# An attention and feed-forward stack on one core: causal tiles of 64 queries with shared products, gates in one run, q and phi k by head block

## The chip, the cores and the metric

One core of a Trainium2 chip runs the whole program. The metric is the time of one execution on the device in microseconds (us). TensorE is called PE here, VectorE DVE, ScalarE ACT, GpSimd POOL, and SyncE, which issues most DMAs, SP.

## What is computed

Four blocks in a row act on x, [2048, 512] in bf16: attention with a memory, a gated feed-forward, and both again with the same weights.

```
x = x + A(layernorm(x));  x = x + B(layernorm(x))      # twice
A: q, k, v = x wq, x wk, x wv         # 32 heads of 16; 4 segments of 512 tokens, one after the other
   a_dot = softmax(q k^T / 4, causal within the segment) v
   a_mem = phi(q) M / (phi(q) z + 1e-6)     # M, z: sums of phi(k) v and phi(k) of the segments before
   A = (g a_mem + (1 - g) a_dot) wo         # g = sigmoid(beta), by head; phi(t) = t + 1 if t > 0, else exp(t)
B: (gelu(x w_gate) * (x w_up)) w_down       # 512 -> 1792 -> 512
```

## The kernel before

A segment of 512 tokens in one pass of attention and feed-forward is a **layer** k; there are 8, k = 0 to 3 the first pass and 4 to 7 the second. The classes `Att` and `Ffn` hold a layer's work as items (q and k by head block b, v by token tile, wo, 14 gates, 14 ups, 4 downs, the memory's update). A head block is 8 heads, 128 of the 512 columns of q; its four groups of 32 partitions hold an even head in the first 16 rows and an odd head in the last 16.

**Scores.** `score_round` makes scores transposed: 128 keys on the partitions, queries in the free dimension, four heads at once in four row strips of PE. For an even head the weights are the 16 rows of k; for an odd head they are 32 rows of `kB`, a copy of k whose even rows are zero. Causal tiles are 128 queries wide: key tile ki meets the 512 - 128 ki queries from 128 ki on, 1280 columns a head, cut by `PIECES` into 5 rounds of 256 columns (`narrow` cuts 128 into 64 for even heads). A **score event** issues two rounds, which fill two pairs of PSUM banks; one exponential on ACT (L1285, 128x1024) empties a pair into a slot of `pt`; POOL zeroes the masked half of the diagonal tile in it (L1291). There are 40 rounds of four heads in a layer and 320 in all.

**Flush.** `flush_item` (L864) multiplies the probabilities of four heads of one parity by v in four column strips of PE. `vaug` holds v with a column of ones times 1/(1 - g) for the denominator. A flush takes 1280 columns and must wait for all masks of its rounds; DVE turns, divides and turns back (L879 to L897), and the slots of `pt` come free.

**Memory.** phi is exp on ACT (L648), a minimum on POOL (L666), a sum on DVE (L652), which for k sums z as well, and a DMA transpose on SP.

**Feed-forward.** A gate is four products of 512 columns. Nine of a layer's 14 are evicted to `gel_sb` by DVE or ACT (L408, L409) and get Gelu later from there (L1046), five get it straight from PSUM (L972); both need a table of ACT other than that of the exponential. DVE multiplies by the ups (L994).

**The order.** All five engines run in an order that `order` writes when the program is built. It keeps a clock for each engine with fixed costs and takes, whenever PE is free, first a score event if two bank pairs and two slots are free and ACT is about to run dry (`rounds_now`), then the open item's next product, then the ready item that is due first. Where nothing is ready it issues a filler product on the tile `warm`, whose result nobody reads. `POLICY` is a table of some forty numbers that shift due times and priorities. PE changes between three modes: row strips (scores, reading the memory), column strips (flush, update, and dense products beside them; L418) and the whole array (dense products, L421). On the chip each engine runs its list in order and waits on semaphores alone.

**Storage.** q, k and `kB` have 3 sets, each of a whole layer, and a layer's projections wait until the scores and phi of the layer three before are done. For k < `kb_dve` = 4 DVE makes kB with a mask (L591); after that SP copies 16 rows of each of four strips by DMA, 4 DMAs a head block (L588). xn, the normalized rows, have 4 buffers and are turned by DMA on SP (L384), or by PE (L509) for three norms.

Of the kernel before, what the change touches and what calls it, by code (L numbers as in the profile page):

```python
# [38 lines left out]
ROUNDS = 5  # L39
STEPS = 8 * ROUNDS  # L40
PIECES = [[(0, 0, 256, 0)], [(0, 256, 256, 0)], [(1, 128, 256, 0)], [(3, 384, 128, 0), (1, 384, 128, 128)],
          [(2, 256, 256, 0)]]
NO_DIAG = 1


def narrow(pieces, par):

    if par:
        return pieces
    return [(ki, q0 + o, min(n, 64) if n == P else n, c0 + o) for ki, q0, n, c0 in pieces  # L50
            for o in ((0, P // 2) if n == P else (0,))]
# [5 lines left out]
SETS = 3  # L57

URGENT, SOON, NORMAL = -4.0, -1.5, 0.0
XN_BUFS = 4  # L60
# [4 lines left out]
POLICY = dict(  # L65
    flush_wait=152.105, piece_slack=40.738, kb_slack=10.905, mem_slack=-2.348, margin=2.56, qk_due=0.594,
    e_q=-0.77, e_k=1.073, exp_slack=-18.49, e_slack=11.096, phi_slack=6.459, gelu_slack=-0.034, act_evict=5.372,
    first_evict=-0.382, gate_step=0.0, up_due=1.256, up_step=0.012, down_due=3.948, down_step=1.013,
    upd_due=-0.62, v0_due=1.254, x1_at=0.158, x2_at=5.744, x3_at=0.964, x3_load=17.129, cut_slack=-0.231,
    direct=5, gelu_tiles=1, phi_pool=0, kb_dve=4, rounds=2, early=0.939, starve=0.658, ahead=0.286, near=-3.652,  # L70
    cap=7, soon=1.448, am_slack=1.081, mem_wait=0.156)
# [11 lines left out]
class Engine:  # L83
# [4 lines left out]
    def __init__(self, overlap=0.0):  # L88
        self.free, self.overlap, self.jobs, self.table = 0.0, overlap, [], "exp"
        self.only, self.rival, self.port = None, None, 0.0  # L90

    def post(self, ready, slack, *steps, table=None, taken=None):

        self.jobs.append((ready, slack, steps, table, taken if taken is not None else []))

# [12 lines left out]
    def serve(self, now):  # L108

        self.jobs = [j for j in self.jobs if not j[4]]  # L110
        jobs = [j for j in self.jobs if not self.only or j[3] in (None, self.only)]
        if not jobs:
            return False
        start = max(self.free, min(j[0] for j in jobs) + self.LATENCY)
# [5 lines left out]
        self.jobs.remove(job)  # L120
        t = ready
# [18 lines left out]
class Clocks:  # L140
# [4 lines left out]
    SWITCH = 0.097  # L145

    def __init__(self):
# [7 lines left out]
        self.ev = {}  # L155

# [19 lines left out]
    def serve(self):  # L176

        again = True
        while again:
            again = False  # L180
            while self.later and self.later[0][0] <= self.pe:
                heapq.heappop(self.later)[2]()
                again = True
            for w in list(self.waiting):
                if w[0]():
                    self.waiting.remove(w)
                    w[1]()
                    again = True
            first = min(self.engines, key=lambda e: max(e.free, min((j[0] for j in e.jobs), default=1e9)))
            again |= first.serve(self.pe) or any(e.serve(self.pe) for e in self.engines)  # L190
# [52 lines left out]

class Box:
# [9 lines left out]
class Policy:  # L254
    def __init__(self, values):
        self.__dict__.update(values)


def order(pol, nc, cst, seg, wrk, psp, A_x, A_wq, A_wk, A_wv, A_wo, A_beta, B_x, B_w_gate, B_w_up, B_w_down, out):
# [70 lines left out]
    bd = cst.tile([P, P], F32, name="bd")  # L330
    nc.gpsimd.memset(bd[:], 1.0)
    nc.gpsimd.affine_select(out=bd[:], in_=bd[:], pattern=[[-16, 8], [0, 16]], compare_op=ALU.is_ge,
                            fill=0.0, base=0, channel_multiplier=1)
    nc.gpsimd.affine_select(out=bd[:], in_=bd[:], pattern=[[16, 8], [0, 16]], compare_op=ALU.is_ge,
                            fill=0.0, base=15, channel_multiplier=-1)
    kBs = [cst.tile([P, KT, L], BF16, name=f"kB{i}") for i in range(SETS)]
    for kB in kBs[1:]:
        nc.vector.memset(kB[:], 0.0)
    mask2 = cst.tile([P, 2 * DH], F32, name="mask2")
    nc.vector.reduce_sum(out=mask2[:], in_=bd[:].rearrange("p (c n) -> p n c", c=4), axis=mybir.AxisListType.X)  # L340
    maskB = mask2[:, DH:DH + 1]

    tmp_e = cst.tile([P, H], F32, name="tmp_e")
    tmp_e2 = cst.tile([P, H], F32, name="tmp_e2")
    cden = cst.tile([P, H], BF16, name="cden")
    macc = cst.tile([P, 4, 2 * DH], F32, name="macc")
    e2x = cst.tile([P, 2, 2, 2, 4 * TPS], F32, name="e2x")
    zacc = cst.tile([P, 4], F32, name="zacc")
    vaugs = [cst.tile([P, TPS, VW + 15], BF16, name=f"vaug{i}")[:] for i in range(SETS)]
    vaugs.append(gel_sb[:].rearrange("p f l -> p (f l)")[:, 0:TPS * (VW + 15)].rearrange("p (t v) -> p t v", t=TPS))  # L350

    def by_head(va):
        return va[:, :, 0:VW].rearrange("p t (h e) -> p t h e", e=DH + 1)


    def gate_constants():
        nc.vector.tensor_scalar(out=cden[:], in0=tmp_e[:], scalar1=1.0, scalar2=None, op0=ALU.add)
        nc.vector.tensor_scalar(out=tmp_e2[:], in0=tmp_e2[:], scalar1=1.0, scalar2=None, op0=ALU.add)

    def gate_rows(half, b):  # L360
        for p in range(2):
            nc.vector.tensor_copy(
# [4 lines left out]

    def later_constants():
        def column(va):
            nc.vector.tensor_copy(out=by_head(va)[:, :, :, DH], in_=cden[:].unsqueeze(1).to_broadcast([P, TPS, H]))  # L370
            nc.vector.memset(va[:, :, VW:], 0.0)

        for n, va in enumerate(vaugs[-1:] + vaugs[:-1]):
            ck.dve.post(12.0 + 3.0 * n, NORMAL, (0.4, lambda va=va: column(va), None))
        for n in range(4):
            ck.dve.post(26.0 + 2.0 * n, NORMAL, (0.25, lambda n=n: gate_rows(*divmod(n, 2)), None))

    def turn_later(t, slack, out, in_, landed, margin=0.0):

        def told(t2):  # L380
            t3 = max(t2 + 1.4 + margin, ck.dma + 1.2)
            ck.at(t3 - 0.2, lambda: landed(t3))

        ck.sp.post(t, slack, (1.3, lambda: nc.sync.dma_start_transpose(out=out(), in_=in_()), told))  # L384
# [49 lines left out]
    class Norm:  # L434
# [4 lines left out]
        def small(self, name, width):  # L439
            return wrk.tile([P, TPS, width], F32, tag=f"{name}{self.key[0]}{self.key[1] % 2}", bufs=1, name=name)  # L440
# [34 lines left out]
        def normed(self, j, i):  # L475
            xn = seg.tile([P, D], BF16, tag=f"xn{i}", bufs=1, name="xn")
            nc.vector.tensor_scalar(out=xn[:], in0=x_sb[:, self.tt0 + j, :], scalar1=self.mv[:, j, 0:1],  # L477
# [3 lines left out]
        def row(self, j, i, ready):  # L481
# [8 lines left out]
            def told(t):  # L490
                if self.key in BY_PE:
                    items.append(self.turn_item(j, xn, t, landed))
                else:
                    turn_later(t, self.slack, lambda: self.xnT[:, :, j * P:(j + 1) * P], lambda: xn()[:], landed,
# [4 lines left out]
        def turn_item(self, j, xn, t, landed):  # L499

            ps = Psum()
            half = L // 2

            def turned():
                return ps()[:, 0:half].bitcast(BF16).rearrange("p (k t) -> p k t", t=P)

            ops = [(Clocks.MM[512] / 2, whole(lambda: nc.tensor.matmul(
                ps()[:, half:L], lhsT=warm[:], rhs=wide[:, 0:2, :], start=True, stop=True)))] * FILL
            ops += [(Clocks.MM[128], whole(lambda kt=kt: nc.tensor.transpose(  # L509
                turned()[:, kt, :], xn()[:, kt * P:(kt + 1) * P], ident[:]))) for kt in range(KT)]  # L510
            return Item(-0.5, lambda: t + Engine.LATENCY <= ck.pe + FILL * Clocks.MM[512] / 2, ops,
# [21 lines left out]
    class Att:  # L533
        def __init__(self, k):
            self.k, self.s, self.tt0 = k, k % NSEG, TPS * (k % NSEG)
            self.norm = Norm(("xnTa", k), self.tt0, f"xnTa{k % 2}", NORMAL, lambda: k < 2 or ("qkv", k - 2) in ev)
            self.vaug = vaugs[(k - 1) % SETS if k else SETS]
            self.ab, self.aT, self.amT, self.n_qkv, self.n_am, self.n_num = {}, None, {}, 0, 0, 0
# [7 lines left out]
        def add_items(self):  # L546
            k, s = self.k, self.s

            def storage():
                return k <= SETS or (("scores", k - SETS) in ev and self.phi_done(k - SETS))  # L550

            def first():
                if k:
                    self.q, self.kf = (seg.tile([P, KT, L], BF16, tag=f"{n}{k % SETS}", bufs=1, name=n)
# [861 lines left out]
```

## Time and profile before

| what | us |
|---|---|
| three runs, median (lowest to highest) | 547.7 (547.62 to 548.58) |
| the profiled execution's own time | 547.77 |
| its span, first to last instruction | 546.1 |
| busy PE, DVE, ACT, POOL | 535.6, 442.4, 445.5, 278.8 |
| exponentials of the scores, 320 | 308.0 |
| masks on POOL, 320 | 184.2 |

The span leaves out what lies around the program, 1.7 us here. A row of the groups reads: line, engine, operation, tiles with shapes, count | busy us, mean ns of one | idle time before, and what ended it. Busy times overlap where an engine starts one instruction before the last has ended. A row of the chain or the timeline reads: start, length, engine, line, tiles, count; matmuls of equal shape and some unequal ones are merged, and the end of the last is modelled. A matmul in strips is counted four times, once a strip.

### The profile page before, as it was taken

How to read it: one execution, taken by the hardware profiler on the slowest of the kernel's cores; microseconds unless marked ns; L12 is line 12 of the kernel's file. 1: busy time of each engine (PE TensorE's matmuls, PEld its weight loads, DVE VectorE, ACT ScalarE, POOL GpSimd, SP SyncE). 2: the span in 40 equal slices, each digit the busy share in tenths (PEclk: the TensorE clock that was granted, in tenths of full speed). 3: DMA queues.
4: the chain of work that ended last, by engine and by line, in shares of the span. 5: the costliest groups of instructions: out<-in, count | busy, mean ns of one | idle time of the engine just before them, and what ended most of it. 6: DMA issues, size and time to landing. Idle time of an engine off the chain costs nothing.

```text
span 546.1 us, 23526 instructions
## 1 busy us (share of the span) xinstructions
PE 535.6 (98%) x10291; PEld 266.0 (49%) x10321; DVE 442.4 (81%) x880; ACT 445.5 (82%) x572; POOL 278.8 (51%) x410
## 2 busy tenths in 40 slices
PE   9999999999999999999999999999999999999997
PEld 4444444445544444444444444455454446445444
DVE  7999999779998999588987987979768796786072
ACT  5899989999999959989999899988998789910500
POOL 2687774367928847156862668724574155300000
PEclk9999999999999999999999999999999999999999
DMA  8248702500150135000224040132201003000001
GB/s 265 46 81 174 178 2 41 166 13 4 30 80 14 42 51 79 12 10 16 42 31 79 13 51 13 31 61 34 53 29 41 18 19 68 4 2 21 21 0 38
DMA packets 66983, 26.96 MB, mean 49 GB/s; under 512 B 55360, under 2 KB 66880, under 8 KB 66880
## 3 DMA queue, kind: packets, MB, share of 16 engines
q1 hardware_dynamic: 66448, 25.19, 22.9%
q8 instruction: 80, 1.31, 1.1%
q10 hardware_dynamic: 432, 0.27, 0.2%
q14 instruction: 23, 0.19, 0.1%
HBM read 9.71 MB, written 2.10 MB: 22 GB/s over the span
## 4 chain that ended last, share of the span: by engine, by line
PE 83%; DVE 12%; issue 2%; DMA 2%; ACT 0%; DVEq 0%
PE ps L418 45%; PE ps L421 21%; PE ps L848 8%; PE ps L864 6%; DVE st L447 1%; DMA phik<-e 1%; DVE byq L879 1%; PE ps L320 1%; DVE x_sb L934 1%; DVE xn L477 1%; DVE ab L887 1%; DMA xnT<-xn 1%; DVE e L652 1%; PE ps L700 1%; DVE gel_sb L408 1%
## 5 line engine op out<-in xcount | busy, mean ns | idle before, releaser
L1285 ACT ACTIVATE pt<-ps 128x1024 bf16<-128x1024 f32 x320 | 308.0, 1026 | 31.4 <-PE ps L848 22.0
L1291 POOL TENSOR_SCALAR_AFFINE_SELECT pt<-pt 128x512 bf16<-128x512 bf16 (+1 forms) x320 | 184.2, 582 | 178.0 <-ACT pt L1285 176.5
L994 DVE TENSOR_TENSOR gel_sb<-gel_sb,ps 128x512 bf16<-128x512 bf16 x112 | 75.4, 685 | 39.4 <-PE ps L421 22.2
L418 PE MATMUL ps<-wd_sb,gel_sb 128*32 128x512 bf16 (+1 forms) x1452 | 81.5, 364 | 0.0
L666 POOL TENSOR_SCALAR e<-e 128x512 bf16<-128x512 bf16 x48 | 73.8, 1541 | 5.1 <-ACT e L648 3.3
L418 PE MATMUL ps<-xnT,wg_sb 128*32 128x512 bf16 x1040 | 63.3, 380 | 0.2 <-DVE gel_sb L408 0.2
L879 DVE STREAM_TRANSPOSE byq<-ps 128x512 f32<-128x512 f32 x64 | 45.4, 709 | 17.4 <-PE ps L864 15.0
L934 DVE TENSOR_TENSOR x_sb<-x_sb,ps 128x512 bf16<-128x512 bf16 (+1 forms) x68 | 43.0, 643 | 16.5 <-PE ps L421 13.4
L418 PE MATMUL ps<-xnT,wu_sb 128*32 128x512 bf16 x956 | 55.3, 380 | 0.0
L418 PEld LDWEIGHTS <-gel_sb 128*32 128x32 bf16 x1452 | 35.9, 96 | 31.3 <-issue 6.5
L421 PE MATMUL ps<-xnT,wu_sb 128*128 128x512 bf16 x202 | 45.9, 379 | 0.7 <-issue 0.3
L421 PE MATMUL ps<-xnT,wg_sb 128*128 128x512 bf16 x178 | 40.9, 379 | 1.0 <-issue 0.5
L864 PE MATMUL ps<-pt,vaug 128*32 128x256 bf16 (+2 forms) x1568 | 40.9, 243 | 0.0
L447 DVE BATCH_NORM_STATS2 st<-x_sb 128x6 f32<-128x512 bf16 x60 | 40.5, 675 | 0.4
L418 PEld LDWEIGHTS <-wg_sb 128*32 128x32 bf16 x1040 | 26.1, 96 | 24.7 <-issue 4.2
L864 PEld LDWEIGHTS <-vaug 128*32 128x32 bf16 x1568 | 32.2, 97 | 10.0 <-issue 1.6
L418 PEld LDWEIGHTS <-wu_sb 128*32 128x32 bf16 x956 | 24.3, 97 | 25.1 <-issue 2.6
L1046 ACT ACTIVATE gel_sb<-gel_sb 128x512 bf16<-128x512 bf16 x63 | 35.0, 632 | 0.0
L418 PE MATMUL ps<-wo_sb,aT 128*32 128x512 bf16 x500 | 31.3, 380 | 0.2 <-DVE x_sb L934 0.2
L421 PEld LDWEIGHTS <-wu_sb 128*128 128x128 bf16 x209 | 19.9, 98 | 23.6 <-issue 0.2
L477 DVE TENSOR_SCALAR xn<-x_sb,mv,rs 128x512 bf16<-128x512 bf16 x64 | 30.2, 526 | 1.2 <-POOL rs L465 0.9
L848 PE MATMUL ps<-q,kf 16*128 16x256 bf16 (+1 forms) x896 | 31.0, 232 | 0.1
(128 smaller groups left out, 718.5 us busy)
## 6 DMA issues: line engine op xcount, KB each, us to landing
wg_sb<-in_B_w_gate_dram SPq DMA_DIRECT2D x8, 224.0 KB, 4.2
wu_sb<-in_B_w_up_dram SPq DMA_DIRECT2D x8, 224.0 KB, 4.1
wd_sb<-in_B_w_down_dram SPq DMA_DIRECT2D x7, 256.0 KB, 4.3
x_sb<-in_A_x_dram SPq DMA_DIRECT2D x3, 512.0 KB, 7.9
out_dram<-x_sb SPq DMA_DIRECT2D x12, 128.0 KB, 1.7
kB<-kf SPq DMA_DIRECT2D x64, 16.0 KB, 1.8
xnT<-xn SPq DMA_TRANSPOSE x48, 2.5
wv_sb<-in_A_wv_dram SPq DMA_DIRECT2D x1, 512.0 KB, 6.9
```

Of the source, the lines that this page charges most:

```text
L418: nc.tensor.matmul(out[r], lhsT=lhsT[:, r], rhs=rhs, start=start, stop=stop, tile_position=(0, 32 * c))
L421: nc.tensor.matmul(out, lhsT=lhsT, rhs=rhs, start=start, stop=stop)
L447: nc.vector.bn_stats(out=self.st6[:, 0, :], in_=x_sb[:, self.tt0 + j, :])
L477: nc.vector.tensor_scalar(out=xn[:], in0=x_sb[:, self.tt0 + j, :], scalar1=self.mv[:, j, 0:1], scalar2=self.rs[:, j, :], op0=ALU.subtract, ...
L666: return lambda: eng.tensor_scalar(out=e[0][:], in0=e[0][:], scalar1=1.0, scalar2=None, op0=ALU.min)
L848: nc.tensor.matmul(ps_all[:, pair[unit // 2], o:o + n], lhsT=lhsT[rows, b, P * ki:P * ki + P], rhs=self.q[rows, b, q0:q0 + n], start=True, ...
L864: nc.tensor.matmul(ps()[32 * j:32 * j + 32, q0:q0 + n], lhsT=self.vaug[:, ki, h * (DH + 1):h * (DH + 1) + 32], rhs=pt_all[:, slot, unit, c ...
L879: nc.vector.transpose(out=self.byq[:, par, :, :].rearrange("p a c -> p (a c)"), in_=ps()[:])
L934: ck.dve.post(ck.made(), slack, (0.15 + 0.00104 * (c1 - c0), lambda: nc.vector.tensor_tensor(out=xt, in0=xt, in1=ps()[:, 0:c1 - c0], op=AL ...
L994: ck.dve.post(ck.made(), NORMAL, (0.683, lambda: nc.vector.tensor_tensor(out=g, in0=g, in1=ps()[:], op=ALU.mult), lambda t: (ps.read(t), e ...
L1285: nc.scalar.activation(out=pt_all[:, s0, :, :].rearrange("p (h u) c -> p h (u c)", h=2), in_=ps_all[:, p0[0]:p0[1] + 1, :], func=ACT.Exp, ...
L1291: nc.gpsimd.affine_select(out=half, in_=half, pattern=[[0, w], [1, P]], compare_op=ALU.is_ge, fill=0.0, base=0, channel_multiplier=-1)
```

## The change

1. **Shared half tiles.** A key tile's first 64 queries see at most its first 64 keys. One product now makes that half tile for two heads: a new tile `kX` has, for each key tile, 64 columns of the even heads' k and then 128 of the odd heads' k; a product with its first 128 columns has the even head's scores on partitions 0 to 63 and the odd head's on 64 to 127. The fifth of now 9 rounds of a pair of heads (`MAIN` = 4) is made of these, four pieces of 64 columns (`SHARED`). The other eight rounds hold the tiles from 64 ki + 64 on. 288 rounds, 288 exponentials, 144 score events.
2. **Values for it.** `vS` holds v of the first 64 tokens of each tile: even heads on partitions 0 to 63, odd heads on 64 to 127, copied from `vaug` by two DMAs a layer. v's heads are stored even first, then odd.
3. **Masks.** Two selects of 64 partitions by 512 for each slot of a shared round, one 64 queries wide for the rest (1386 and 1380).
4. **kX.** One tile a head block for all layers; its copy for layer k waits for the scores of layer k-1 of that block. DVE makes it for k < 3 (two maskings), SP after that, 8 DMAs a head block.
5. **Ring.** q and k lie in a ring of 12 head blocks; a projection waits for the block 12 before.
6. **Gates in one run.** `direct` = 14: the first gate makes the other 13 the most urgent items and holds scores and phi back until all are issued; each gets Gelu straight from PSUM.
7. z is summed by the update's product (its column of ones) and no longer on DVE; constants are made on POOL; fillers are 128 columns, those ahead of a PE transpose 32; xn has 3 buffers; layer 1's xn is turned by PE; `POLICY` has other numbers throughout, and the planner's costs changed a little.

```diff
-PIECES = [[(0, 0, 256, 0)], [(0, 256, 256, 0)], [(1, 128, 256, 0)], [(3, 384, 128, 0), (1, 384, 128, 128)],
-          [(2, 256, 256, 0)]]
+PIECES = [[(0, 64, 256, 0)], [(0, 320, 192, 64), (3, 448, 64, 0)], [(1, 192, 256, 0)],
+          [(2, 320, 192, 0), (1, 448, 64, 192)]]
+SHARED = [(ki, P * ki, Q, Q * ki) for ki in range(KT)]
...
-            for ki, q0, n, c0 in narrow(PIECES[i], par):
+            for ki, q0, n, c0 in SHARED if par is None else PIECES[i % (MAIN + 1)]:
                 for j in range(4):
...
+                    rows = slice(32 * j, 32 * j + (16 if par == 0 else 32))
+                    if par == 0:
+                        lhsT = self.kf[b]()[rows, P * ki:P * ki + P]
+                    elif par:
+                        lhsT = kXs[b][rows, ki, Q:]
+                    else:
+                        lhsT = kXs[b][rows, ki, 0:P]
...
+                work = [(r + (MAIN + 1) * par, self.vaug, piece) for r in range(MAIN) for piece in PIECES[r]]
+                work += [(MAIN, self.vS, piece) for piece in SHARED]
...
+                    for n in range(8):
+                        ck.sp.post(t, slack, (0.78, copy(n % 4, n // 4), sent if n == 7 else None))
...
+                    ck.when(lambda: k == 0 or ("sc", k - 1, b) in ev, lambda: masked(max(t, ck.pe) if k else t))
...
+                    if pol.direct >= FT:
+                        if self.n_gate == 1:
+                            ck.burst = FT
+                            for it in items:
+                                if it.kind == "gate" and it.after == ("xnTf", k):
+                                    it.due = -0.8
+                        ck.burst -= 1
+                        ck.act.post(ck.made(), pol.burst_slack, (0.602, lambda: nc.scalar.activation(
+                            out=gel_sb[:, ft, :], in_=ps()[:], func=ACT.Gelu_apprx_tanh),
...
-        if not streams or not rounds_ready(2):
+        if not streams or not rounds_ready(2) or ck.burst > pol.hold:
             return 0
...
-                product(ps(), warm[:], wide)
+                product(ps()[:, 0:P], warm[:], warm[:])
```

Where the order shows it. On ACT, around the gates of layer 1, before (gel_sb<-gel_sb is Gelu on an evicted gate, gel_sb<-ps at L409 an eviction and at L972 Gelu from PSUM):

```order
L409 ACTIVATE gel_sb<-ps 128x512 x3
L648 ACTIVATE e<-kf 128x512
L409 ACTIVATE gel_sb<-ps 128x512 x2
L648 ACTIVATE e<-kf 128x512
L409 ACTIVATE gel_sb<-ps 128x512
L1285 ACTIVATE pt<-ps 128x1024 x2
L648 ACTIVATE e<-kf 128x512
L1046 ACT_TABLE_LOAD
L1046 ACTIVATE gel_sb<-gel_sb 128x512
L972 ACTIVATE gel_sb<-ps 128x512 x3
```

and the same place now:

```order
L1376 ACTIVATE pt<-ps 128x1024 x4
L455 ACTIVATE xnT<-ps 128x4x128
L734 ACTIVATE e<-q 128x512
L455 ACTIVATE xnT<-ps 128x4x128
L1376 ACTIVATE pt<-ps 128x1024 x2
L1044 ACT_TABLE_LOAD
L1044 ACTIVATE gel_sb<-ps 128x512 x14
L1376 ACT_TABLE_LOAD
L1376 ACTIVATE pt<-ps 128x1024 x8
```

The evictions of gates between exponentials are gone, and all 14 Gelus stand between two table loads with no exponential among them.

On SP, the masked copies of k of layer 4, before:

```order
L588 DMA kB_121<-kf 16x512 x4
L384 DMA_TRANSPOSE xnT<-xn 128x4x128 x4
L588 DMA kB_121<-kf 16x512 x12
L384 DMA_TRANSPOSE amT<-am 128x4x128 x2
L384 DMA_TRANSPOSE xnT<-xn 128x4x128 x4
```

and now (kX_120 and kX_121 are the first two head blocks, vS the shared values, amT the memory's part of the attention, turned):

```order
L644 DMA kX_120<-kf 16x4x64 x4
L644 DMA kX_120<-kf 16x4x128 x4
L430 DMA_TRANSPOSE xnT<-xn 128x4x128 x3
L430 DMA_TRANSPOSE phik<-e 128x4x128
L430 DMA_TRANSPOSE xnT<-xn 128x4x128
L680 DMA vS_125<-vaug_136 64x4x272 x2
L644 DMA kX_121<-kf 16x4x64 x4
L644 DMA kX_121<-kf 16x4x128 x4
L430 DMA_TRANSPOSE amT<-am 128x4x128 x4
```

A head block has eight copies where it had four, whole blocks stand ahead of the transposes of xn and of am, and the fourth transpose of xn stands apart from the first three.

More of the change, by code (lines that the diff above doesn't have):

```diff
@@ L1099, in order @@
     first_scale(2, 4)
+    gate_constants()
+    for va in vaugs[-1:] + vaugs[:-1]:
+        column(va)
     n0.first_xn = [n0.normed(0, 0), n0.normed(1, 1)]
@@ L1104, in order @@
     a0 = att[0]
-    a0.made()
     half = L // 2
@@ L1201, in rounds_now @@
         wait = backlog()
-        if pol.rounds > 2 and n >= 3 and left != 4 and wait < pol.ahead and rounds_ready(3):
-            return 3
-        if n >= 2 and left != 3 and (idle or left in (2, 4) or wait < (pol.early if streams[0][0] < 1 else pol.starve)):
+        if n >= 2 and (idle or left == 2 or wait < (pol.early if streams[0][0] < 1 else pol.starve)):
             return 2
```

420 lines of the change are left out of this document (239 added, 181 removed).

## The prediction

> **What bounds the kernel now.** First the page: span, busy shares, and the chain that ended last, by engine.
>
> ```profile
> span 546.1 us, 23526 instructions
> ## 1 busy us (share of the span) xinstructions
> PE 535.6 (98%) x10291; PEld 266.0 (49%) x10321; DVE 442.4 (81%) x880; ACT 445.5 (82%) x572; POOL 278.8 (51%) x410
> ...
> PE 83%; DVE 12%; issue 2%; DMA 2%; ACT 0%; DVEq 0%
> ```
>
> TensorE has matmuls in flight for 98% of the span, and the chain lies on it for 83%. A busy PE may still be spaced out, so I looked next at the table of stretches (cut near the layers) and at who waits.
>
> ```profile
> 182.00:245.00 63.00, 62.34 (x1308) 30.17 (x1308) 53.86 (x106) 53.55 (x68) 33.15 (x49) 1.00 0.24 40
> ```
>
> This is the fourth of nine stretches; the columns behind the length are PE, PEld, DVE, ACT and POOL, then the granted clock, which is full. PE is busy 62.34 of 63 us, ACT and DVE some 54. The waits say the same:
>
> ```profile
> ACT pt L1285 <- PE ps L848: 22.0, 34, 3.8
> ...
> PE ps L421 <- issue: 1.7, 11, 0.2
> PE ps L320 <- DVE warm L313: 1.1, 1, 1.1
> ```
>
> The exponentials wait 22.0 us for score products, while PE's longest sums of waiting are 1.7 and 1.1 us. So PE's own instruction stream is the bound: a change gains what it takes out of this stream, and loses the waits that it puts in. Work saved on ScalarE, VectorE and GpSimd counts only where PE waits for it.
>
> **Prices on PE.** The ends of pipelined matmuls are modelled, so I price by the distance from start to start in the timeline of PE, and by one long run of the chain.
>
> ```profile
> 251.09 0.40 PE L848 MATMUL ps<-q,kB 32*128 32x256 bf16 x8
> 251.42 0.62 PE L418 MATMUL ps<-wv_sb,xnT 128*32 128x512 bf16 x8
> 251.86 0.73 PE L864 MATMUL ps<-pt,vaug 128*32 128x256 bf16 x32
> 252.41 0.61 PE L418 MATMUL ps<-wo_sb,aT 128*32 128x512 bf16 x8
> 252.95 0.40 PE L848 MATMUL ps<-q,kB 32*128 32x128 bf16 x12
> ...
> 256.76 0.72 PE L864 MATMUL ps<-pt,vaug 128*32 128x256 bf16 x24
> 257.31 1.04 PE L418 MATMUL ps<-wv_sb,xnT 128*32 128x512 bf16 x16
> ```
>
> And from the chain in order of time:
>
> ```profile
> 473.65 25.04 PE ps L418 x464
> ```
>
> - A product of 512 columns: 464 matmuls in four column strips are 116 products; 25.04 / 116 = 0.216 us. By that rate 256 columns are 0.108, 128 are 0.054, 64 are 0.027.
> - A score event has two rounds of 256 columns: 0.33 us from 251.09 to 251.42. The columns are 0.216 of it, so leaving the row strips costs about 0.11. Entering costs the same: from 252.41 to 252.95 are 0.54 us, two products are 0.432.
> - A flush (the probabilities of four heads times their values) has 1280 columns. It took 0.55 us (251.86 to 252.41) with 32 matmuls, four of its eight groups only 64 wide, and 0.55 us (256.76 to 257.31) with 24 matmuls in six wider groups. So cutting columns into 64s costs nothing that shows here.
>
> **The change on PE.** The order of before and after is counted, then priced.
>
> 1. Scores. Two heads share the products of the half tiles, so a pair of heads has 9 rounds of 256 columns and not 10: 288 rounds for 320. 32 x 0.108 = **-3.5 us**.
> 2. Changes between row strips, column strips and the whole array: 351 before, 321 after, since there are 144 score events for 160. 30 x 0.11 = **-3.3 us**.
> 3. Filler products on the warm tile. The rows are
>
> ```profile
> L418 PE MATMUL ps<-warm 128*32 128x512 bf16 x76 | 5.0, 381 | 0.0
> L509 PE MATMUL ps<-ident,xn 128*128 128x128 bf16 x48 | 4.8, 219 | 0.0
> L507 PE MATMUL ps<-warm 128*128 128x256 bf16 x24 | 4.8, 275 | 0.8 <-DVE q L408 0.8
> ```
>
>    Before: 76 / 4 = 19 products of 512 columns in strips and, by the order, 9 over the whole array (6.0 us) and 24 of 256 (2.6). After, from the order: 93 of 128 columns (5.0) and 32 of 32 columns; no 32-wide one is in this trace, by columns it is 0.013, by the 64-wide group 0.027; I take 0.027 as the nearest row (0.9). **-2.7 us**.
> 4. Transposes of xn on PE: 48 become 64 (L509's row), as layer 1's go over PE too: 16 x 0.054 = **+0.9 us**.
> 5. The flush keeps its 1280 columns, in ten groups, six of them 64 wide. By the two equal flushes above: 0. The dense products of the projections and the feed-forward are the same number: 0.
>
> Sum: -3.5 - 3.3 - 2.7 + 0.9 = **-8.6 us**. The profiled execution took 547.77 us (546.1 of span and 1.7 around it; the median is 547.7), so 547.8 - 8.6 = 539.2 us.
>
> The upper end of point 5, and of the scores: if a 64-wide group cost as much as a 128-wide one, the 384 groups by which they increase (256 before, 640 after) would cost 384 x 0.027 = +10.4. The trace has row-strip loads of 32 rows only beside wider products; I take 0, since the 32-matmul flush is the nearest row.
>
> **The change on the other engines.** It must not put a wait into PE's stream.
>
> ```profile
> L1285 ACT ACTIVATE pt<-ps 128x1024 bf16<-128x1024 f32 x320 | 308.0, 1026 | 31.4 <-PE ps L848 22.0 <-POOL pt L1291 5.1 <-PE ps L418 1.1
> L1291 POOL TENSOR_SCALAR_AFFINE_SELECT pt<-pt 128x512 bf16<-128x512 bf16 x192 | 128.6, 676 | 88.7 <-ACT pt L1285 88.2
> ...
> L1291 POOL TENSOR_SCALAR_AFFINE_SELECT pt<-pt 128x256 bf16<-128x256 bf16 x128 | 55.9, 440 | 89.3 <-ACT pt L1285 88.3 <-DVE rdm L718 0.5
> ...
> L1046 ACT ACTIVATE gel_sb<-gel_sb 128x512 bf16<-128x512 bf16 x63 | 35.0, 632 | 0.0
> ...
> L408 DVE CAST gel_sb<-ps 128x512 bf16<-128x512 f32 x35 | 23.2, 681 | 4.6 <-PE ps L418 4.5
> ...
> L972 ACT ACTIVATE gel_sb<-ps 128x512 bf16<-128x512 f32 x35 | 19.6, 594 | 0.3 <-PE ps L418 0.2
> ```
>
> ScalarE loses 32 exponentials (308.0 / 320 = 0.96 each, 31 us), some 10 evictions of about L972's 0.594, and 63 x 0.038 by Gelu from PSUM (0.594 for 0.632): about 39 us. VectorE loses 33 gate casts of 0.681 (23 us) and gets a second masking of k in 16 blocks, half as wide as the first. GpSimd goes from 184.5 us of masks to 224 x 0.440 + 64 x 0.32 (half way down from 0.676 over 0.440) + 128 x 0.676 = 206 us, and takes the constants. It spent 177 us waiting for exponentials, so I cost this at nothing; without that cover a flush would start one extra select, 0.68 us, later. None of these gains enters the sum, since PE did not wait there.
>
> Two things are tighter. The first is **the run of gates**: between the exponentials there is now one stretch in which PE makes 14 gates, 14 x 4 x 0.216 = 12.1 us, with no scores.
>
> ```profile
> 149.88 1.94 ACT L1285 ACTIVATE pt<-ps 128x1024 bf16<-128x1024 f32 x2
> ...
> 161.24 1.28 ACT L1285 ACT_TABLE_LOAD   x1
> 162.53 1.94 ACT L1285 ACTIVATE pt<-ps 128x1024 bf16<-128x1024 f32 x2
> ```
>
> Before, the exponentials paused 10.7 us (151.8 to 162.5). After, the pause is at least the gates and the table load behind them, 12.1 + 0.6 + 1.3 = 14.0: 3.3 us more in each of 7 layers, 23 us. The 39 us saved cover it. The second is **SP's queue**, whose rows are two of its timeline and one of its waits, below. The masked copy of k is now made by 8 DMAs a head block, not 4, in layers 3 to 7 (160 for 64), with 16 more for the shared values.
>
> ```profile
> 241.32 12.70 SPq L588 DMA_DIRECT2D kB<-kf  x16
> ```
>
> ```profile
> 352.44 5.91 SPq L384 DMA_TRANSPOSE xnT<-xn  x4
> ```
>
> ```profile
> SPq L384 <- DVE xn L477: 108.7, 12, 27.6
> ```
>
> One such issue is 12.70 / 16 = 0.79 us, one transpose 1.48. The extra 112 issues are 89 us on a queue whose transposes stood 108.7 us waiting for xn alone, so it fits on the whole. In the order the copies now stand right ahead of and between the transposes of xn and am; who is late then is the transpose, and PE's projections behind it. I take 0, as a block's copies are wanted only in its fifth round.
>
> **Rivals.**
> - *The relief also removes waits.* The two sums of PE's waits quoted are 2.8 us, and each other is shorter. If all went, some -4: **535 us**. Against it: most are not for ScalarE or VectorE.
> - *SP's queue becomes the wait (slower).* In layers 3 to 7 the four extra copies of one head block stand ahead of the next layer's xn transposes and nothing else is ready on PE: 5 x 4 x 0.79 = +15.8, **555 us**. It decides from 8.6 / 5 = 1.7 us, two copies, in each layer. For it: the order puts whole blocks there. Against it: the wait of 108.7 us and the dense products that PE has as a reserve.
> - *PE waits at the end of the gate run.* Scores that fill PSUM cannot leave before the table is back: 7 x 1.28 = +9, **548 us**, about no change. Against it: 14 up products, 12.1 us, are ready just then.
> - *The narrow groups cost*: weights of a 64-wide group load no faster than they stream, +10.4, **549.6 us**. The two flushes speak against it. The Trainium skill, "TensorE: Matmul & The Clock Gate", section "Back-to-back issue gap", has a rule for it: in a stream of weight loads and matmuls the spacing at 128 columns is some 81 ns, not the 56 ns of an isolated matmul. By that, 25 ns for each of 384 added groups would be an estimated +9.6 us and the gain gone; the trace's 0.55 us for both flushes disagrees with it for strips.
>
> **How the numbers follow.** Forecast 0.57 (own range 535.5 to 543.5: the unpriced 32-wide fills, and waits that move by some 4 us either way); more gained 0.13; SP 0.13; gate run 0.10; narrow groups 0.07. A measurement of this kernel can tell 0.2%, 1.1 us, from no change. Faster by more: 0.57 + 0.13 and a third of the last two, which can come in part, 0.76. Same: 0.05. Slower: the SP case and a third of those two, 0.19. The range reaches from the gaining rival, taken with the 32-wide fills at nothing and a microsecond of rounding (533), over the gate run and the narrow groups to 551, and leaves out the SP case.
>
> **What would show it.** In the profile after: 288 exponentials; a score event, shared round or not, still 0.33 us from start to start; a flush of 40 matmuls 0.55 us (0.70 would mean that narrow groups cost); a PE busy share of 98% again. Waits of PE's projections for xnT, or of L920 for kX, beyond 5 us together show the SP case; a wait of 1.3 us for exponentials behind each gate run the third rival. The forecast is wrong if the waits in PE's stream grow by more than the 8.6 us.

## The result and the profile after

The changed kernel takes 545.0 us (544.86 to 546.64, 4 runs) where the kernel before takes 548.0 beside it (547.62 to 548.58, 4 runs): ratio 0.9951, 95% interval 0.9930 to 0.9973, a gain of 3.0 us. Two later comparisons of the same pair on other chips gave 546.01 for 547.80 (0.9958, 0.9943 to 0.9972) and 545.55 for 547.61 (0.9962, 0.9948 to 0.9976). So the change gains about 2 to 3 us, the forecast was 8.6. The direction was right and the time lies in the range, but more than half of the gain isn't there. The profiled execution is the slowest of its four, 546.64.

The page of the kernel after: span, TensorE, and, from its third part, the queue that brings code (packets, MB, share). Below it the same queue row of the kernel before, which the prediction didn't look at.

```profile
span 544.9 us, 26532 instructions
## 1 busy us (share of the span) xinstructions
PE 532.0 (98%) x11698; PEld 292.5 (54%) x11698; DVE 407.4 (75%) x786; ACT 415.8 (76%) x530; POOL 310.5 (57%) x530
...
q8 instruction: 91, 1.49, 1.2%
```

```profile
q8 instruction: 80, 1.31, 1.1%
```

PE still has matmuls in flight for 98% of the span, with 3.6 us less of them and 1377 more weight loads. A packet of q8 is 1.49 MB / 91 = 16 KB. Each product is a weight load and a matmul, so by the weight loads PE has 23,396 instructions after and 20,642 before; 91 and 80 packets are one for each 257 and 258 of them.

Two of the marks that the prediction set, from the groups of the kernel after and its timeline of PE (start, length, line, out<-in, shape, count):

```profile
L1376 ACT ACTIVATE pt<-ps 128x1024 bf16<-128x1024 f32 x288 | 275.0, 1027 | 33.7 <-PE ps L920 25.9 <-POOL pt L1380 4.6 <-POOL pt L1386 1.1
```

```profile
30.43 0.40 PE L920 MATMUL ps<-wd_sb,kX 32*128 32x256 bf16 x12
30.76 0.40 PE L464 MATMUL ps<-xnT,wq_sb 128*32 128x512 bf16 x4
...
71.34 0.62 PE L464 MATMUL ps<-xnT,wq_sb 128*32 128x512 bf16 x8
71.90 0.28 PE L920 MATMUL ps<-q,kf 16*128 16x192 bf16 x5
73.05 0.21 PE L920 MATMUL ps<-q,kf 16*128 16x64 bf16 x3 [0.88 <-issue]
...
260.68 0.62 PE L937 MATMUL ps<-pt,vaug 128*32 128x256 bf16 x24
261.12 0.29 PE L937 MATMUL ps<-pt,vS 128*32 128x64 bf16 x16
261.24 1.04 PE L464 MATMUL ps<-wv_sb,xnT 128*32 128x512 bf16 x16
```

There are 288 exponentials. A score event takes 0.33 us (30.43 to 30.76), and a flush of 40 matmuls 0.56 (260.68 to 261.24), where 0.70 would have meant that narrow groups cost. So the prices held. What is new stands at 71.90: in the middle of a round, between two products of the same tiles, PE stands for 0.88 us, and the trace finds nothing that it waits for ("issue"). The list of PE's waits in the kernel after has more of them (sum, times, longest):

```profile
PE ps L464 <- DMA wd_sb<-in_B_w_down_dram: 1.4, 1, 1.4
...
PE ps L937 <- issue: 1.0, 1, 1.0
PE ps L920 <- issue: 0.9, 1, 0.9
PE ps L937 <- DVE byq L951: 0.7, 1, 0.7
PE ps L464 <- ACT pt L1376: 0.6, 2, 0.3
PE ps L937 <- POOL pt L1380: 0.5, 1, 0.5
PE ps L464 <- issue: 0.5, 1, 0.5
PE ps L854 <- issue: 0.4, 1, 0.4
```

With a last one of 0.2 the "issue" rows are 3.0 us. From start to start, less the product's own time, they are 3.8. The kernel before has an issue row too, 1.7 us in 11 pieces, but it is no wait: each is at most 0.2 long, one product's time, and that trace has 30 matmul records fewer than weight loads. Counting PE's instructions from the start of the trace after, and reading its DMA records for the last 16 KB packet of q8 that landed before PE went on, shows what the five have in common:

```
start us   wait us   number of the instruction   its place in a block of 256   packet landed us   PE goes on us
 27.54      0.34        962                       194                           26.40              27.93
 71.99      1.03       3265                       193                           71.68              73.05
141.80      1.17       6337                       193                          141.75             143.06
375.74      0.57      17602                       194                          374.94             376.34
463.07      0.68      21697                       193                          462.38             463.86
```

PE goes on 1.3 to 1.5 us after a packet has landed, each time. For the short issue pieces of the kernel before, that distance is anything from 0.5 to 10.6 us.

**The theory** that this suggests: PE's code comes in blocks of 256 instructions, and a stretch of many short products runs through a block faster than the next one arrives. The change cuts work into narrower products, so it has less work and more instructions. **The rivals**: the waits belong to the new order of the plan and its late operands; SP's queue; narrow groups that cost more than they show.

### The profile page after: what moved, and what is told of

Read it like the earlier page. It is cut to its first block, busy times and chain, and to the rows that moved or that the text cites. A ratio compares the mean times of both kernels' runs of the same rounds, so it can differ in the third digit from the quotient of the medians.

```text
span 544.9 us, 26532 instructions
## 1 busy us (share of the span) xinstructions
PE 532.0 (98%) x11698; PEld 292.5 (54%) x11698; DVE 407.4 (75%) x786; ACT 415.8 (76%) x530; POOL 310.5 (57%) x530
## 3 DMA queue, kind: packets, MB, share of 16 engines
q8 instruction: 91, 1.49, 1.2%
## 4 chain that ended last, share of the span: by engine, by line
PE 84%; DVE 8%; DMA 2%; POOL 2%; issue 2%; ACT 1%; SPq 0%; DVEq 0%; POOLq 0%
PE ps L464 47%; PE ps L467 22%; PE ps L920 7%; PE ps L937 6%; DMA wd_sb<-in_B_w_down_dram 1%; DVE x_sb L1007 1%; DMA phik<-e 1%; DVE st L493 1%; POOL pt L1380 1%; PE ps L556 1%; DVE e L738 1%; DVE q L454 1%; DVE vaug L454 1%; DVE byq L951 1%; POOL pt L1386 1%
## 5 line engine op out<-in xcount | busy, mean ns | idle before, releaser
L1376 ACT ACTIVATE pt<-ps 128x1024 bf16<-128x1024 f32 x288 | 275.0, 1027 | 33.7 <-PE ps L920 25.9
L1380 POOL TENSOR_SCALAR_AFFINE_SELECT pt<-pt 128x256 bf16<-128x256 bf16 (+1 forms) x288 | 118.2, 422 | 134.2 <-ACT pt L1376 128.1
L1386 POOL TENSOR_SCALAR_AFFINE_SELECT pt<-pt 64x512 bf16<-64x512 bf16 x128 | 92.0, 719 | 4.2
L464 PE MATMUL ps<-wd_sb,gel_sb 128*32 128x512 bf16 (+1 forms) x1424 | 81.6, 365 | 2.2 <-DMA wd_sb<-in_B_w_down_dram 1.4
L464 PE MATMUL ps<-xnT,wu_sb 128*32 128x512 bf16 x1372 | 81.8, 380 | 0.0
L751 POOL TENSOR_SCALAR e<-e 128x512 bf16<-128x512 bf16 x48 | 73.8, 1545 | 4.0 <-ACT e L734 2.3
L1044 ACT ACTIVATE gel_sb<-ps 128x512 bf16<-128x512 f32 x98 | 56.5, 599 | 25.2 <-PE ps L464 15.3
L464 PEld LDWEIGHTS <-wu_sb 128*32 128x32 bf16 x1372 | 38.1, 96 | 27.6 <-issue 0.2
L464 PEld LDWEIGHTS <-gel_sb 128*32 128x32 bf16 x1424 | 37.0, 96 | 27.4 <-issue 2.5
L464 PE MATMUL ps<-xnT,wg_sb 128*32 128x512 bf16 x876 | 49.6, 379 | 0.0
L920 PEld LDWEIGHTS <-kX 32*128 32x128 bf16 x1280 | 19.2, 92 | 33.9 <-issue 33.4
L464 PEld LDWEIGHTS <-wg_sb 128*32 128x32 bf16 x876 | 27.5, 97 | 17.3
L467 PEld LDWEIGHTS <-wg_sb 128*128 128x128 bf16 x229 | 22.0, 98 | 25.9 <-issue 0.2
L920 PE MATMUL ps<-q,kX 32*128 32x64 bf16 (+2 forms) x1120 | 31.3, 217 | 0.0
```

The costliest lines, as they stand in the source:

```text
L464: nc.tensor.matmul(out[r], lhsT=lhsT[:, r], rhs=rhs, start=start, stop=stop, tile_position=(0, 32 * c))
L467: nc.tensor.matmul(out, lhsT=lhsT, rhs=rhs, start=start, stop=stop)
L751: return lambda: eng.tensor_scalar(out=e[0][:], in0=e[0][:], scalar1=1.0, scalar2=None, op0=ALU.min)
L920: nc.tensor.matmul(ps_all[:, pair[unit // 2], o:o + n], lhsT=lhsT, rhs=self.q[b]()[rows, q0:q0 + n], start=True, stop=True, tile_position= ...
L1044: ck.act.post(ck.made(), pol.burst_slack, (0.602, lambda: nc.scalar.activation(out=gel_sb[:, ft, :], in_=ps()[:], func=ACT.Gelu_apprx_tanh ...
L1376: nc.scalar.activation(out=dst, in_=src, func=ACT.Exp, scale=SCALE)
```

## Experiments

**1. The kernel before with narrower score products.** Nothing but the count of instructions changes; each product's weights and columns in all are the same.

```diff
-            for ki, q0, n, c0 in narrow(PIECES[i], par):
+            for ki, q0, n, c0 in [(k, q + o, min(m, 64), c + o)
+                                  for k, q, m, c in narrow(PIECES[i], par) for o in range(0, m, 64)]:
```

> The kernel before, its order untouched, with every score product cut into products 64 columns wide: some 6660 more PE instructions, and by the measured 29 ns for four 64-wide strips only 1.9 us more work. Code supply (the theory: PE's code comes in blocks of 256 instructions that cannot follow each other closer than about 3.3 us, and denser stretches stand without a semaphore): +1.9 and some 4 to 5 us of such waits, 553.5 to 555.5, all at one place of the 256. The plan's own waits (rival: the waits after the change belong to its new order, and the count of instructions is no matter): 549.9, no new waits. Narrow groups cost (rival: 25 ns for each of 832 added groups): 569.

559.81 us, +11.7 (ratio 1.0217, 1.0199 to 1.0234). Its waits of PE, its timeline at the longest, and the stretch behind that one (length, PE, PEld, DVE, ACT, POOL, granted clock, DMA share, GB/s):

```profile
PE ps L848 <- issue: 3.1, 3, 2.2
...
PE ps L418 <- issue: 1.8, 4, 0.7
PE ps L864 <- issue: 1.6, 2, 1.3
```

```profile
64.18 0.32 PE L848 MATMUL ps<-q,kB 32*128 32x64 bf16 x18
66.69 0.40 PE L848 MATMUL ps<-q,kB 32*128 32x64 bf16 x14 [2.20 <-issue]
```

```profile
66.70:73.00 6.30, 6.30 (x122) 3.09 (x125) 3.93 (x9) 4.39 (x5) 2.93 (x4) 0.51 0.02 5
```

The order of before, which had no such wait, now has nine over 0.4 us, 8.6 us from start to start, all between places 167 and 189 of the 256 (missing records let the place slide down over the run). PE goes on 1.2 to 1.6 us behind a packet in all of them. One of the nine, 1.0 us at 471.7, stands in the list as a wait for GpSimd's masks: where a semaphore happens to come just then, the list gives its name. Behind the longest the granted clock was 0.51 for 6.3 us, so some 3 us more went there. 1.9 + 8.6 + 3 comes to the +13.6 of its span (559.7 for 546.1), closer than the estimates in it deserve. Narrow groups (569) and the plan's own waits (549.9) both miss; code supply had the mechanism and half of its size, and hadn't thought of the clock.

**2 and 3. Two strips in place of four, in the kernel before and after.** The dense products that share a mode with the flush get half the instructions.

```diff
-            for c in range(4):
-                r = slice(32 * c, 32 * c + 32)
-                nc.tensor.matmul(out[r], ..., tile_position=(0, 32 * c))
+            for c in range(2):
+                r = slice(64 * c, 64 * c + 64)
+                nc.tensor.matmul(out[r], ..., tile_position=(0, 64 * c))
```

> The kernel before with the dense products that it makes as four strips of 32 outputs made as two strips of 64 instead: 5220 PE instructions fewer. Both theories: the kernel before has no waits for code, so nothing is won by it; this is the control of the next run and prices the strips. If going between strips of 32 and of 64 is a change of mode, 91 more of them cost 9 us, 557; if not, 548.

> The kernel after with the same edit: two strips of 64 for four of 32 in dense products and fillers, 5580 PE instructions fewer, the order the same. Code supply: the waits without a semaphore (some 4 us) go, so the time against the kernel after stands 4 us lower than the edit's effect on the kernel before: 541 if the strips cost nothing, 550 if they cost 9. The plan's own waits: the same effect as on the kernel before, 545 or 554.

Before: 556.02, +7.9 (1.0142, 1.0126 to 1.0159). After: 551.91 (1.0066, 1.0053 to 1.0078), which is 6.4 over the 545.5 that the kernel after takes in the middle of its three comparisons. Going between strips of 32 and 64 is a change of mode: 91 more of them for 7.9 us are 0.087 each. Its trace shows the same from start to start: 0.10 us (median) at each such change, while a product of 512 columns in two strips still takes 0.216. In the changed kernel the edit is 1.5 us cheaper than in the kernel before, and 2 us if one allows for the changes that the traces count (93 more before, 99 after). That is the direction of the theory but not its 4 us. Its waits say 2: of the 3.0 us of issue one of 0.9 is left, beside missing records.

```profile
PE ps L920 <- issue: 0.9, 1, 0.9
```

**4. The late weight.** The wait for wd_sb, 1.4 us, was PE's longest. The loads are made due 20 us earlier, which puts them ahead of the phi k transposes on SP.

```diff
-        late_pieces.append((94.0 + 2.0 * h, 256, lambda r=r: load(
+        late_pieces.append((74.0 + 2.0 * h, 256, lambda r=r: load(
```

> The kernel after with the loads of w_down due 20 us earlier in the plan, so that the last ones stand on SP ahead of the phi k transposes; no other engine's order moves. Code supply and late waits: the wait of 1.4 us of a down product for wd_sb goes and about that is won, 543.6, the waits without a semaphore stay. If the waits of the plan only move (rival): 545.0.

545.37 (0.9945, 0.9931 to 0.9958): no gain that can be told from the 545.0 to 546.0 of the kernel after, so the rival's 545.0 came nearer than 543.6. The row for wd_sb is gone from PE's waits. (A row of 1.2 us for GpSimd's L751 is new in them, at 141 us; it stands at the product and place of the 1.17 us wait for code and is that wait under another name.) The same wait is also short or absent in two of the other runs of that order, below, so it is one that comes and goes; it isn't where the 5 to 6 us went.

**5 and 12. The kernel after once more**, on two other chips.

> The kernel after once more, unchanged, for its scatter and for a second profile. Code supply: 545, with waits of PE that have no semaphore at the same places of the 256 instructions and about the same places of the program, 3 to 4.5 us together; their lengths move by some tenths with what the DMA engines do at that moment. Rival (late operands by chance): other places.

> The kernel after, unchanged, on the chip of the run before it, as its measure: 545 to 546, waits without a semaphore of 3 to 4.5 us as in its two profiles.

546.01 and 545.55, as told above. In their traces the waits without a semaphore are 4.1 and 2.2 us from start to start, the second below the 3 to 4.5 expected. The first of these traces has all five of the first profile's and one more at 69 us; the second has three of the five, at 27.6, 140.7 and 374.6. Their places go from 194 down to 172 as records go missing. So the place belongs to the code, but how long each wait is, and whether it comes, changes from run to run, and the kernel's times spread more (543.99 to 546.77 in eight runs) than the loss of any one of them.

**6. Every instruction half a block further on.** 128 PE instructions are put ahead of the first work.

```diff
-    keep_warm(WARM, 0)
+    keep_warm(WARM - 4, 0)
+    for _ in range(68):
+        nc.tensor.matmul(ps_all[:, 0, 0:32], lhsT=warm[:], rhs=warm[:, 0:32], start=True, stop=True)
```

> The kernel after with 128 more PE instructions ahead of its first work (68 products 32 wide in place of 4 that are 512 wide, while PE has nothing to do), so that every later instruction stands half a block of 256 further on. Code supply: the waits without a semaphore stay at the same place of the 256 and so move to other lines and times; the waits for semaphores stay where they were; 543 to 547. Rival (waits of the plan or of the operands): all waits stay at their lines and times; 545.

545.46 (0.9956, 0.9943 to 0.9969). The waits without a semaphore are now at 25.68 us (1.50), 61.97 (1.01), 67.35 (0.59) and 207.22 (0.52), at places 193, 192, 190 and 184, and PE goes on 1.2 to 1.4 us behind a packet each time. None is left at 72, 142, 376 or 463 us. The first in the timeline (line numbers are two higher here), inside a score round where the kernel after had none:

```profile
25.67 0.26 PE L922 MATMUL ps<-wd_sb 16*128 16x192 bf16 x4
27.26 0.32 PE L922 MATMUL ps<-wd_sb 16*128 16x64 bf16 x8 [1.33 <-issue]
```

The waits for semaphores stayed where they were: that for byq is 0.9 at 50.4 us for 0.9 at 49.1, those for GpSimd's masks are at 200.2 and 203.3 for 201.0 and 204.1. The one kind follows the count, the other the program.

**7. The rate by itself.** Two streams behind the kernel's last work wait for nothing.

```diff
+    for n, wide_n in ((512, Q), (256, UNIT)):
+        for g in range(n):
+            for j in range(4):
+                r = slice(32 * j, 32 * j + 32)
+                nc.tensor.matmul(ps_all[r, g % 4, 0:wide_n], lhsT=warm[:, r],
+                                 rhs=warm[:, 0:Q] if wide_n == Q else wide[:, 0:2, :], start=True, stop=True,
+                                 tile_position=(0, 32 * j))
```

> The kernel after with two streams of products on PE behind its last work, with no operand to wait for and idle DMA engines: 512 groups of four strips 64 wide (16 blocks of 256 instructions), then 256 groups of four strips 256 wide (8 blocks). Code supply: a block of the first takes about 3 us whatever it holds, 45 to 50 us in all, with PE standing at each boundary; a block of the second holds 32 x 0.109 = 3.5 us of work and so comes without waits, 28 us. No limit on code: 512 x 0.029 = 14.8 us and 28 us. Weight load sets narrow groups: 512 x 0.054 = 28 us without standing.

One execution, 631.78 us. Its timeline of PE, the stretch of the first stream (columns as above), and the DMA view from 543 to 560 us:

```profile
547.13 1.90 PE L1462 MATMUL ps<-warm 128*32 128x64 bf16 x128 [2.80 <-issue]
550.60 1.90 PE L1462 MATMUL ps<-warm 128*32 128x64 bf16 x128 [1.57 <-issue]
...
594.45 2.54 PE L1462 MATMUL ps<-warm 128*32 128x64 bf16 x128 [1.57 <-issue]
598.19 30.59 PE L1462 MATMUL ps<-warm 128*32 128x256 bf16 x1009 [1.21 <-issue]
```

```profile
547.13:594.45 47.32, 24.68 (x1665) 22.58 (x1666) 0.00 (x0) 0.00 (x0) 0.00 (x0) 0.50 0.02 5
```

```profile
q8 instruction: 5, 0.08, 2.0%
```

Each row of x128 is one block: 128 matmuls and as many weight loads. 13 of them take 47.32 us, 3.64 each, and PE stands 1.57 us or more before each. The five packets in 17 us are the only traffic, 16 KB each, one a block. The whole narrow stream took 55 us for the 45 to 50 expected. The wide stream, 3.49 us a block at full clock (from 604.0 us on), shows no wait in the 30.59 us after its first. So code comes at 3.64 us a block in the narrow stream, and in no trace here do two packets start less than 3.28 us apart: a stretch stalls when block after block holds less work than that. In the kernel after the 256 instructions from 22.4 us on went by in 2.3 us without a wait, and the next 256 ended in the wait at 27.54, so some code is held ahead; the limit is one of stretches. The clock had fallen to 0.50 in the narrow stream, which is why its blocks are 1.90 of busy time. The low clock doesn't seem to be what made the code slow: the one block that ran at full clock all through, from 543.11 on, was busy for 1.22 us, and the next began 4.02 us after it.

The Trainium skill, "Runtime: NRT & Kernel Launch", section "Instruction fetch mechanics", says that code is refilled in 16 KiB blocks of 256 instructions; the packets agree. It also says that crossing into the next block is mostly hidden. With 64-wide strips the trace disagrees: 1.57 us and more at each.

**8. The masked k on VectorE in all layers**, which takes all 160 of its DMAs off SP: `'kb_dve': 3` becomes `'kb_dve': 8` in the plan's numbers, and the plan is made anew.

> The kernel after with the masked copy of k made on VectorE in all layers, so that SP issues none of its 160 copies; the plan is made anew, its PE work is 0.4 us more and 250 instructions fewer. SP's queue as the loss (rival): most of the 5 us comes back, 540 to 541. Code supply and late operands: SP is not at fault; 545 within 2 us, VectorE's waits a little longer.

547.38 (0.9994, 0.9983 to 1.0006), no faster than before, and 0.4 us outside the 545 within 2 that was expected. The order is another one here, so this run alone doesn't clear SP's queue; that PE has no wait for xnT or kX in the list of the kernel after does. In its place VectorE is later (the first row; the second is the late weight again):

```profile
PE ps L937 <- DVE byq L951: 1.5, 2, 0.8
PE ps L464 <- DMA wd_sb<-in_B_w_down_dram: 1.5, 1, 1.5
```

**9 and 10. No fillers.** The third term of the prediction counted 2.7 us of fillers saved. Here the main loop's fillers are left out, with the plan's clock and order as they are.

```diff
-                product(ps(), warm[:], wide)
+                ck.tiling("columns" if ck.mode == "columns" or ck.mode == "rows" and any(
+                    it.kind == 'flush' for it in items) else "whole")
```

> The kernel before without the 28 filler products that the plan puts in where it finds no work for PE (19 in strips, 9 over the whole array, 512 wide, 6.0 us); the order of the rest of PE's work is the same. If a filler only covers a wait for an operand, PE waits in its place and the time stays, 547.8, within 1; if the operands were there (the prediction's third term took it so), the 6.0 us go, 542.

> The kernel after without its 93 filler products of 128 columns (5.0 us, 528 PE instructions); the order of the rest of PE's work is the same. Fillers cover waits: 545.5, within 1, with new waits for semaphores of 4 to 5 us. Fillers are plain work: 540.5. Code supply adds to either some tenths of gain, for 2% fewer instructions.

Before without them: 548.88, +1.1 (1.0016, 1.0005 to 1.0026), just beyond the "within 1". 6.0 us of products were taken out and nothing was won. Its timeline and stretches show where they went:

```profile
20.67 0.40 PE L848 MATMUL ps<-wd_sb 32*128 32x128 bf16 x12
23.30 1.26 PE L864 MATMUL ps<-pt,gel_sb 128*32 128x256 bf16 x32 [2.24 <-DVE gel_sb L408]
```

```profile
16.60:20.60 4.00, 4.00 (x80) 1.63 (x68) 3.93 (x12) 4.00 (x7) 2.28 (x5) 1.00 0.01 2
...
23.30:33.00 9.70, 8.54 (x132) 3.65 (x136) 9.26 (x26) 7.04 (x8) 6.76 (x12) 0.50 0.29 45
```

PE waits 2.24 us for VectorE in the fillers' place, and then runs at half clock for 9.7 us. So a filler covers a wait and holds the clock. After without them: 543.76 (0.9917, 0.9898 to 0.9936), 1.2 to 2.3 us under the kernel after in its three comparisons, and the fastest median of this study; neither 545.5 nor 540.5. It has waits for operands in the fillers' place, as the kernel before has without its fillers,

```profile
22.48 0.74 PE L937 MATMUL ps<-pt,gel_sb 128*32 128x256 bf16 x40
24.92 0.49 PE L920 MATMUL ps<-wd_sb 16*128 16x192 bf16 x12 [1.70 <-ACT pt L1376]
```

and the clock fell here too, to 0.50 for 6.8 us. But its waits for code fell to about 1.0 us, in three pieces: 57 fillers in four strips (8 instructions each) and 36 over the whole array (2 each) are 528 instructions.

**11. The same fillers in a quarter of the products.** Four of 128 columns become one of 512: the same time on the warm tile, 398 instructions fewer.

```diff
-                product(ps()[:, 0:P], warm[:], warm[:])
+                if len(ck.fills) % 4 == 3:
+                    product(ps(), warm[:], wide)
+                else:
+                    ck.tiling(...)
```

> The kernel after with each four of its fillers of 128 columns made as one of 512: the same time on the warm tile (23 for 93), 398 PE instructions fewer, all between 22 and 141 us, the rest of PE's order the same. Code supply: the waits without a semaphore lose what they lost in the kernel without fillers (about 2 us), and the clock does not fall as it did there, so 542 to 544, no slower than without fillers. Rival (the kernel without fillers won by plain work left out): 545.5, as the kernel after.

544.05 (0.9942, 0.9923 to 0.9961), 1.5 us under the kernel after on the same chip (545.55); the two intervals overlap, so this gain is likely and not settled, and the times spread from 542.58 to 548.04. The profiled execution took 542.92. Its waits of PE hold no row of issue at all; the first two and the last are

```profile
PE ps L464 <- DMA wd_sb<-in_B_w_down_dram: 1.5, 1, 1.5
PE ps L341 <- DVE warm L334: 1.1, 1, 1.1
...
PE ps L464 <- DVE x_sb L1007: 0.2, 1, 0.2
```

Nothing was left out of the work here, so what went is the waits for code. But not all of it is owed to fewer instructions. The fillers stand at 22 to 29 and at 140 to 141 us. The waits at 376 and 463 us lie behind them all and went because the blocks now begin 142 instructions further on in the program (398 - 256), as in experiment 6 they begin elsewhere. In experiment 10, where the shift there is only 16 (528 - 512), waits stayed at 373 and 460 us (0.25 and 0.45), while the one at 142 us, right behind 15 fillers of 8 instructions, was gone. How much of the gain each of the two is worth isn't shown. That the clock stays (1.00 from 22 to 32 us) doesn't bring the time under that of the kernel without fillers: this is the part of the expectation that missed.

## Why the prediction was wrong, step by step

- **What bounds the kernel: right.** PE is busy for 98% before and after, and the relief of ScalarE (445.5 to 415.8 us busy, 30 us and not the 39 worked out) and VectorE (442.4 to 407.4) did not shorten PE's waits: without the issue rows 4.5 us before, 6.2 after.
- **Scores, -3.5: held in count and price.** 288 rounds, 0.33 us an event.
- **Changes of mode, -3.3: right in count, somewhat large in price.** The traces count the same 351 and 321. 91 added ones, between strips of 32 and 64, cost 0.087 each in the kernel before; 30 at that price are 2.6.
- **Fillers, -2.7: mis-sized.** They were priced as work, but they stand where PE would wait. Taking 6.0 us of them out of before gave +1.1. What counts is fillers and waits together: before 8.6 + 4.5, the latter by the list of PE's waits without its issue rows, after 5.9 + 6.2; that is -1.0, not -2.7.
- **Narrow groups at nothing: right for the array.** Flush and score events kept their times. The rival that priced them by weight load is refuted at the kernel's own widths.
- **The step that failed: "It must not put a wait into PE's stream", with a sum that took in no new wait.** The prediction sought it on the other engines alone, and the new wait was PE's own code: PE does not wait on semaphores alone, as the description of the kernel has it. The 2754 more instructions made dense stretches of a few blocks in 91; in three profiles of the kernel after they cost 3.8, 4.1 and 2.2 us. Shown by the packets that land 1.2 to 1.7 us before PE goes on, by instructions added to before (1), by the waits that move with the count (6) and by the rate alone (7); that they end when fillers get wider (11) fits, with the caveat given there. The prediction's own sign, waits that grow by more than 8.6 us, was too wide to catch a loss of this size.
- The sum by what was measured: -3.5 - 2.6 - 1.0 + 0.9 = -6.2; with 2.2 to 4.1 us of waits for code -4.0 to -2.1. The three comparisons gave -3.0, -1.8 and -2.1. Taken profile by profile, against the span of 546.1 before, the sum with each one's own waits is -2.4, -2.1 and -4.0, and the spans of 544.9, 545.0 and 543.1 gave -1.2, -1.1 and -3.0. The remaining microsecond is within what the terms are known to, and I can't put it to a place.
- **SP's queue, 0.13, and the end of the gate run, 0.10: neither came.** PE has no wait for xnT, nor L920 for kX in the list of the kernel after; all its waits of L464 for exponentials are 0.6 us. Off SP, the masked k was slower (8).
- **Not settled:** why the 1.4 us for wd_sb come in some runs and not in others, how far ahead code is held, and how the gain of experiment 11 divides between fewer instructions and the place at which the blocks begin.

## What to carry to other kernels

When a change turns wide products into more narrow ones, count PE's instructions as well as its columns: here blocks of 256 that held less than some 3.3 to 3.6 us of work, one after another, could stall, and a wait named "issue" that recurs at one place of 256, behind a 16 KB packet, is the sign of it. Which stretch stalls depends on where the blocks begin, so a hundred instructions more or less ahead of it can move the wait. Price fillers together with the waits that they cover, never as work that can be saved. Make fillers few and wide; here that likely took off 1.5 us.

## What the runs showed of the hardware

- Code reaches PE in packets of 16 KB, 256 instructions each. In a stream of products 64 columns wide that waits for nothing else a block takes 3.64 us, with PE standing 1.57 us or more at each boundary and going on 1.2 to 1.5 us after the packet has landed. Two packets never start less than 3.28 us apart in these traces.
- The clock gave way after waits shorter than I had thought: 2.20 us of standing in experiment 1 were followed by 0.51 for 6.3 us, 2.24 us in experiment 9 by 0.50 for 9.7 us, 1.70 us in experiment 10 by 0.50 for 6.8 us. The Trainium skill, "TensorE: Matmul & The Clock Gate", section "What's actually happening", gives an idle window of about 3.4 us before the clock falls. The trace of experiment 9 disagrees: PE was busy for 4.00 of the 4.00 us that end half a microsecond before the gap, and the gap is shorter than that. The waits of up to 1.4 us in the kernel after were not followed by a fall: its mean clock was 1.0. Where the clock fell, it stayed at half for 10.24 us (experiment 9) or 6.83 us (1 and 10) by its own records, three and two times 3.41.
- Strips of 32 and of 64 outputs are different modes: 0.087 us of the whole time for each added change between them, 0.10 from start to start.
